# Attention values turned by DMA for the last six units, and q loaded in pairs of rows: one step in a chunked-attention and bilinear-FFN kernel

## The chip, the cores and the metric

One core of a Trainium2 chip runs the whole program in one launch. The metric is device time in microseconds (us). The kernel before was timed three times.

## The reference

The program computes attention inside chunks of 64 tokens, and feeds it to a bilinear feed-forward layer. All inputs and the output are float32; the kernel computes in bfloat16 with float32 sums.

```python
batch, n_heads, seq, head_dim = (8, 8, 576, 64)
chunk = 64; nc = S // chunk; scale = 1.0 / np.sqrt(D)
# q_c, k_c, v_c = q, k, v reshaped to (B, H, nc, chunk, D)
scores = scale * np.matmul(q_c, k_c.transpose(0, 1, 2, 4, 3))
scores = scores - np.max(scores, axis=-1, keepdims=True)
attn = np.exp(scores)
attn = attn / (np.sum(attn, axis=-1, keepdims=True) + 1e-09)
out = np.matmul(attn, v_c)                     # back to (B, H, S, D)
x = out.transpose(0, 2, 1, 3).reshape(B * S, H * D)   # 4608 tokens x 512
return (x @ w_a) * (x @ w_b) @ w_out           # 512 -> 1536 -> 512
```

## The kernel before

The 4608 tokens are cut into 9 blocks of 512 tokens (K = 0 to 8) and 18 units of 256 tokens (u = 0 to 17, two to a block, four chunks of 64 to a unit). Block 4 collects the last chunk of every sequence, so its tokens lie apart in DRAM; in the other blocks a unit is 256 tokens of one sequence.

**Attention of a unit.** `load_natural` (line 449) fetches q, k and v as tokens by heads, in DRAM runs of 64 float32 (256 bytes), two loads of 128 tokens to each tensor. `cast_natural` and `cast_v` make bfloat16 of them. One DMA transpose on SP (`turn_dma`, line 652) turns q and k of a unit, 128 x 2048 elements, into `qkT`, with head columns on partitions. Three pieces of TensorE (PE) work follow, all as 64 x 64 tiles of the PE array, four side by side:

- `part_scores` (line 781): 32 matmuls with a chunk of k as the weights and a chunk of q as the moving operand, and two exponentials on ScalarE (ACT) that write `E`.
- `part_sums` (line 739): four matmuls of 512 columns with a matrix of ones, which spread the sum of each softmax row over 64 partitions; ACT then takes the logarithm of both halves (line 745) and the exponential of its negative (line 747), which gives `inv`, the reciprocals.
- `part_values` (line 752): 32 matmuls with v as the weights and `E` moving. The product has model columns on partitions and tokens along the free dimension, as the FFN wants it, and VectorE (DVE) multiplies it by `inv` straight into `xT` (line 772).

Units 0 to 3 go through functions of their own with pairs of heads (`load_pair`, `cast_pair`, `turn_pair` and so on).

**FFN of a block.** Block 0 is done plainly (`ffn`). Blocks 1 to 8 go through `side_group` (three groups to a block, lines 882 to 995), which replaces eight block products by seven with sums of operands: `x_sums` (line 864) adds and subtracts quarters of `xT`, `product` (line 907) makes four matmuls of 256 columns on weights or weight sums, and ACT, DVE and GpSimd (POOL) combine the results into `AB`. `out_seven` (line 1185) does the same for the last matrix, and `out_last` (line 1036) for block 8. `store` (line 1015) and `send` (line 1086) write the output, a store of 128 tokens at a time, on SP's DMA queue, or at the very end also on ACT's.

**Order.** Every step is an operation with its dependences in a `Planner`. Which engine takes it, in what order, and which of the eight PSUM banks it uses is written out by hand in one long table, `ORDER_OF_ALL` (line 85), that `follow` reads: `a` is PE, `b` ACT, `c` DVE, `d` POOL, `e` the SP queue; the digits after a colon are banks; `f` is a fill matmul on zeros that only keeps PE running. The program order in the functions is thus not the order on the engines. In the table the 64-row work of the units stands in groups of adjacent steps between the FFN products; between the two kinds PE changes its tiling mode.

From block 5 on (`JOINT`), `attend_two` (line 1436) hands out the attention of two units at three places inside `out_seven`: sums of the first with scores of the second; values of the first with sums of the second; values of the second with scores of the next.

## Time and profile before

| | |
|---|---|
| median of three runs | 292.86 us (292.47 to 293.28) |
| the profiled execution | 292.49 us |
| its span, first to last instruction | 290.7 us |
| granted TensorE clock | 1.000 |
| busy: PE, DVE, POOL, ACT | 285.5, 246.2, 185.9, 176.2 us |
| DMA moved | 55.09 MB in 137176 packets, 122160 of them under 512 bytes |

The span is shorter than the time by what lies before the first and after the last instruction. A busy share says how long an engine had work, not whether that work set the end; for that one reads which engine the last chain runs through, and the timeline.

### The profile page before, as it was taken

What the parts mean: (1) busy time and instruction counts of PE and PEld (TensorE: products, weight loads), DVE (VectorE), ACT (ScalarE), POOL (GpSimd) and SP (SyncE); (2) the same over time, 40 slices, a digit from 0 to 9 for tenths busy, and PEclk for the clock granted to TensorE, in tenths of its full rate; (3) what the DMA queues carried; (4) which work ended last, traced back from release to release, by engine and by line L of the source; (5) the groups of instructions that cost most, each with busy time, mean ns of one, the idle gap of its engine ahead of it and who ended that gap; (6) DMA issues with size and microseconds to landing.
All of it is one profiled execution on the core that took longest, in us unless ns stands there. A gap on an engine that the chain in (4) does not pass through costs nothing.

```text
span 290.7 us, 8704 instructions
## 1 busy us (share of the span) xinstructions
PE 285.5 (98%) x3549; PEld 233.4 (80%) x3549; DVE 246.2 (85%) x433; ACT 176.2 (61%) x307; POOL 185.9 (64%) x180
## 2 busy tenths in 40 slices
PE   7999999999999999999999999999999999999995
PEld 3455458887887888788888878888888888888884
DVE  2778899998999998998988988779988889688583
ACT  3887977966667654866683496558827642332521
POOL 4641338465498298539899879967743685787530
PEclk9999999999999999999999999999999999999999
DMA  7999999899767899976999997997950120012034
GB/s 252 390 398 402 288 297 317 195 244 236 177 132 176 226 242 208 271 167 153 211 244 191 251 220 211 205 243 166 160 116 2 40 106 2 0 68 79 3 145 145
DMA packets 137176, 55.09 MB, mean 189 GB/s; under 512 B 122160, under 2 KB 128432, under 8 KB 137136
## 3 DMA queue, kind: packets, MB, share of 16 engines
q1 hardware_dynamic: 135904, 53.43, 71.9%
q10 hardware_dynamic: 1232, 1.11, 1.1%
q8 instruction: 27, 0.44, 0.6%
q14 instruction: 13, 0.11, 0.1%
HBM read 37.75 MB, written 9.44 MB: 162 GB/s over the span
## 4 chain that ended last, share of the span: by engine, by line
PE 95%; DMA 3%; DVE 0%; POOL 0%; issue 0%; ACT 0%; ACTq 0%
PE F L911 51%; PE F L1216 25%; PE F L822 7%; DMA f<-in_k_dram 3%; PE F L1054 3%; PE F L685 2%; PE F L723 2%; PE F L695 2%; PE F L1529 1%; PE F L501 1%; PE F L630 0%; PE F L579 0%; PE F L673 0%; PE F L550 0%; PE F L710 0%; POOL qkb L326 0%
## 5 line engine op out<-in xcount | busy, mean ns | idle before, releaser
L326 ACT COPY part<-F 128x512 f32<-128x512 f32 x91 | 52.5, 591 | 52.0 <-PE F L911 36.2
L945 POOL TENSOR_TENSOR AB<-AB,bsb 128x512 bf16<-128x512 bf16 x46 | 52.8, 1155 | 21.0 <-DVE wst L1173 7.2
L949 DVE TENSOR_TENSOR bsb<-F,part 128x512 bf16<-128x512 f32 x72 | 49.1, 684 | 8.0 <-PE F L911 4.8
L1173 POOL TENSOR_TENSOR wst<-AB 128x512 bf16<-128x512 bf16 x30 | 34.3, 1155 | 13.4 <-PE F L1216 9.9
L911 PEld LDWEIGHTS <-WA 128*128 128x128 bf16 x384 | 37.1, 98 | 5.5 <-issue 1.1
L911 PEld LDWEIGHTS <-WB 128*128 128x128 bf16 x384 | 37.6, 98 | 4.6
L326 ACT COPY wst<-F 128x512 f32<-128x512 f32 (+1 forms) x40 | 22.1, 557 | 29.7 <-PE F L1216 17.9
L949 DVE TENSOR_TENSOR AB<-F,part 128x512 bf16<-128x512 f32 x48 | 32.8, 684 | 2.0 <-PE F L911 1.4
L1216 PEld LDWEIGHTS <-wst 128*128 128x128 bf16 x288 | 28.0, 98 | 3.7 <-issue 0.4
L1216 PEld LDWEIGHTS <-AB 128*128 128x128 bf16 x288 | 28.1, 98 | 3.5 <-issue 0.2
L911 PEld LDWEIGHTS <-Tb 128*128 128x128 bf16 x288 | 27.6, 98 | 3.9 <-issue 0.5
L911 PEld LDWEIGHTS <-Ta 128*128 128x128 bf16 x288 | 27.7, 98 | 3.6 <-issue 0.3
L911 PE MATMUL F<-wst,Tb 128*128 128x256 bf16 x192 | 28.9, 273 | 0.0
L911 PE MATMUL F<-wst,Ta 128*128 128x256 bf16 x192 | 28.9, 273 | 0.0
L911 PE MATMUL F<-xT,WA 128*128 128x256 bf16 x192 | 28.9, 273 | 0.0
L911 PE MATMUL F<-wst,WA 128*128 128x256 bf16 x192 | 28.8, 273 | 0.0
L911 PE MATMUL F<-wst,WB 128*128 128x256 bf16 x192 | 28.8, 273 | 0.0
L911 PE MATMUL F<-xT,WB 128*128 128x256 bf16 x192 | 28.3, 273 | 0.0
L326 POOL CAST qkb<-f 128x1024 bf16<-128x1024 f32 (+1 forms) x21 | 17.2, 835 | 15.1 <-DVE Tb L859 6.3
L1216 PE MATMUL F<-WO,AB 128*128 128x256 bf16 x192 | 24.6, 273 | 0.0
L326 DVE COPY part<-F 128x512 f32<-128x512 f32 x29 | 19.8, 686 | 2.7 <-PE F L911 2.3
L772 DVE TENSOR_TENSOR xT<-F,inv 128x512 bf16<-128x512 f32 x28 | 18.0, 684 | 2.6 <-ACT inv L747 2.1
(135 smaller groups left out, 561.2 us busy)
## 6 DMA issues: line engine op xcount, KB each, us to landing
f<-in_q_dram SPq DMA_DIRECT2D x32, 256.0 KB, 4.8
f<-in_v_dram SPq DMA_DIRECT2D x32, 256.0 KB, 4.3
f<-in_k_dram SPq DMA_DIRECT2D x28, 256.0 KB, 4.5
out_dram<-osb SPq DMA_DIRECT2D x28, 256.0 KB, 3.2
wst<-in_moe_w_b_dram SPq DMA_DIRECT2D x6, 512.0 KB, 8.4
wst<-in_moe_w_a_dram SPq DMA_DIRECT2D x6, 512.0 KB, 8.7
wst<-in_moe_w_out_dram SPq DMA_DIRECT2D x6, 512.0 KB, 6.1
out_dram<-osb SPq DMA_DIRECT2D x12, 128.0 KB, 2.4
```

Of the source, the lines that this page charges most:

```text
L326: return A.copy(out=out, in_=in_) if e == "act" else ENG[e].tensor_copy(out=out, in_=in_)
L685: T.matmul(PS[j][cl * 64:cl * 64 + 64, c:c + 64], chunk_of(u, 1, m, j, 2 * g + cl), chunk_of(u, 0, m, j, 2 * g + cl), start=True, stop=True,)
L695: T.matmul(SU[cl][j * 64:j * 64 + 64, :], ones[cl * 64:cl * 64 + 64, :], E[u % 2][cl * 64:cl * 64 + 64, j, :], start=True, stop=True,)
L723: T.matmul(PA[cl][j * 64:j * 64 + 64, c:c + 64], vb[u % 2][cl * 64:cl * 64 + 64, g * 512 + h * 64:g * 512 + h * 64 + 64], E[u % 2][cl * 64 ...
L772: op("dve", c_dve(512), lambda e, cl=cl: V.tensor_tensor(out=x.rearrange("p m (g c t) -> p c g m t", g=2, c=2)[:, cl], in0=f_of(PA[cl]).re ...
L822: T.matmul(f_of(b)[:, 0:n].rearrange("p (u t) -> p u t", u=len(us)), w[ft][:, kt, :], x[:, us[0]:us[-1] + 1, kt, :], start=(kt == 0), stop ...
L911: T.matmul(f_of(bank)[:, q * 256:q * 256 + 256], lhs(2 * g + q, kt), rhs[:, kt, :], start=(first and q == 0 and kt == 0), stop=(q == 1 and ...
L945: op(("dve", "pool"), TIMES, lambda e: ENG[e].tensor_tensor(out=dst, in0=dst, in1=b, op=MULT), r=bk, w=key, prio=-300, fast=True)
L949: op("dve", c_dve(512), lambda e: V.tensor_tensor(out=dst, in0=two(f_of(bank)), in1=two(pab[s][i]), op=ADD), r=[("ps", id(bank)), ("part", ...
L1054: T.matmul(f_of(bank)[:, 0:256], lhs[:, i, h], rhs[:, i, :], start=(first and i == 0), stop=(i == NP - 1), skip_group_check=True)
L1173: op(*long_op(hs), lambda e, i=i, x=x, y=y, o_=o_: ENG[e].tensor_tensor(out=SS[i][:, s], in0=x[:, s], in1=y[:, s], op=o_), r=fts + [(name, ...
L1216: T.matmul(f_of(bank)[:, at:at + 256], lhs[:, i, tt * 128:tt * 128 + 128], rhs[:, i, :], start=(first and at == 0 and i == 0), stop=(i == ...
```

## The change

Two edits, and an order written anew.

1. For units 12 to 17 (`FROM = 12`, blocks 6 to 8) `part_sums` and `part_values` give way to `part_first` and `part_second`, each for half of the heads. The operands are swapped: a chunk of `E` is the weights and v is moving, so the product has tokens on partitions and model columns along the free dimension. `vb` gets a 65th column of ones beside each head's 64, so each matmul has 65 columns and the last is the sum of the softmax row. DVE takes the reciprocal of four sums to a partition and multiplies 256 columns by them into `xk`, which lies in the memory of `inv`; that is four reciprocals and four products to a unit. When both units of a block are done, `turn_x` turns 128 x 2048 elements into `xT` by one DMA transpose on SP. The tokens of a unit then stand in another order inside `xT` (chunk of the pair outermost), and `rows_of` writes them back in place: a store of 128 partitions goes to two groups of 64 rows in DRAM, 128 rows apart.
2. For units 4 to 17 q is loaded with two neighbouring tokens to a partition (`load_paired`), in DRAM runs of 512 bytes and in one load to a unit (four in block 4). The cast puts the two tokens in two halves of `qkb`, the same DMA transpose turns it, and `chunk_of` reads a chunk's 64 columns of q as 32 pairs, the two of a pair 512 elements (1,024 bytes) apart. k and v are loaded as before.
3. `ORDER_OF_ALL` is another table from its fifth step on. Steps by engine, before and after: PE without fills 580 and 580, ACT 311 and 298, DVE 432 and 460, POOL 172 and 175, SP 192 and 183, fills 25 and 24. The order of the first dozen loads on SP is the same.

The diff without the table and without lines that only rename:

```diff
@@ -215,7 +215,8 @@
     STORES = {}
     ORDER = "P0 P1 P2 P3 V0 V1 X0 q2 k2 X1 v2 X2 k3 q3 v3 O0 O1 O2 O3 O4 O5"
     JP = (0,4,7)
-    INVERSES = 2
+    FROM = 12
+    PAIRED = {(u, 0) for u in range(4, 18)}
     QT = 2
     JOINT = 4
     JOINT_SPARE = 1
@@ -271,22 +272,23 @@
 
     f32 = [[buf(f"f32_{i}_{x}", [128, 1024], FP32) for x in range(3)] for i in range(NF32)]
     qkb = [buf(f"qkb_{i}", [128, 2, 1024], BF16) for i in range(2)]
-    vb = [buf(f"vb_{i}", [128, 1024], BF16) for i in range(2)]
+    vb = [buf(f"vb_{i}", [128, 16, 66], BF16) for i in range(2)]
     qkT = [buf(f"qkT_{i}", [128, 16, 128], BF16) for i in range(QT)]
+    rec = [buf(f"rec_{i}", [128, 4, 4], FP32) for i in range(2)]
     E = [buf(f"E_{i}", [128, 2, 512], BF16) for i in range(2)]
 
     part = buf("part", [128, 3, 512], FP32)
-    inv = [buf("inv", [128, 2, 512], FP32), part[:, 0:2]] + [buf(f"inv_{i}", [128, 2, 512], FP32) for i in range(INVERSES - 1)]
-
-    def NI(u):
-
-        return 0 if u % INVERSES == 0 else 2
     xT = [buf(f"xT_{i}", [128, 2, NKT, 256], BF16) for i in range(NX)]
     AB = [buf(f"AB_{i}", [128, NP, 2, BLK], BF16) for i in range(2)]
     NB = 8
     bsb = buf("bsb", [128, NB, BLK], BF16)
     NO = 3
     osb = [buf(f"osb_{i}", [128, 2, DM], FP32) for i in range(NO)]
+    inv = [buf("inv", [128, 2, 512], FP32), part[:, 0:2], buf("inv_1", [128, 2, 512], FP32)]
+    xk = [inv[2 * i].rearrange("p a b -> p (a b)").bitcast(BF16).rearrange("p (u c) -> p u c", u=2) for i in range(2)]
+
+    def NI(u):
+        return 0 if u % 2 == 0 else 2
 
     WA = buf("WA", [128, NFT, NKT, 128], BF16)
     WB = buf("WB", [128, NFT, NKT, 128], BF16)
@@ -446,6 +451,27 @@
             return [(0, 128, b0, s0)]
         return [(0, 64, b0, s0), (64, 64, b1, s1)]
 
+    def load_paired(u, x, src):
+
+        t = f32[u % NF32][x].rearrange("p (h c) -> p h c", h=H)
+        (b, s0), (b1, _) = chunks[4 * u], chunks[4 * u + 1]
+        if b == b1:
+            load(t, src[b, :, s0:s0 + 256, :].rearrange("h (p r) d -> p h (r d)", r=2), f_keys(u, x), (1024, 24.0))
+            return
+        for n in range(4):
+            b, s0 = chunks[4 * u + n]
+            load(t[32 * n:32 * n + 32], src[b, :, s0:s0 + 64, :].rearrange("h (p r) d -> p h (r d)", r=2), f_keys(u, x, n), (256, 24.0))
+
+    def rows_of(u, tt, cols):
+
+        if u < FROM:
+            return [(p, n, out[b * S + s0:b * S + s0 + n, cols]) for p, n, b, s0 in runs(u, tt)]
+        (b0, s0), (b1, s1) = chunks[4 * u + tt], chunks[4 * u + 2 + tt]
+        if b0 == b1 and s1 == s0 + 128:
+            r0 = b0 * S + s0 - 64 * tt
+            return [(0, 128, out[r0:r0 + 256, cols].rearrange("(g c t) d -> c g t d", g=2, c=2)[tt])]
+        return [(64 * g, 64, out[b * S + s0:b * S + s0 + 64, cols]) for g, (b, s0) in enumerate(((b0, s0), (b1, s1)))]
+
     def load_natural(u, x, src, prio=None):
         t = f32[u % NF32][x]
         for g in range(2):
@@ -603,7 +629,7 @@
 
     def cast_v(u, engs, prio):
         cost = {"dve": 0.69, "pool": 1.04, "act": 1.05}
-        op(engs, [cost[e] for e in engs], lambda e: copy(e, vb[u % 2], f32[u % NF32][2]), r=f_keys(u, 2), w=vb_keys(u % 2), prio=prio, fast=True)
+        op(engs, [cost[e] for e in engs], lambda e: copy(e, vb[u % 2][:, :, 0:64], f32[u % NF32][2].rearrange("p (n d) -> p n d", n=16)), r=f_keys(u, 2), w=vb_keys(u % 2), prio=prio, fast=True)
 
     def v_rows(K, half):
         return osb[K].rearrange("p t c -> p (t c)").bitcast(BF16)[:, half * 1024:half * 1024 + 1024]
@@ -640,25 +666,37 @@
                 hs = (half,) if K in BY_HALF else (0, 1)
                 c = slice(256 * hs[0], 256 * hs[-1] + 256)
                 n = 256 * len(hs)
-                op(("act", "dve"), (c_act(n), c_dve(n)), lambda e, g=g, c=c: copy(e, vb[g // 2][:, g % 2 * 512:g % 2 * 512 + 512][:, c], f_of(VB[g])[:, c]),
+                op(("act", "dve"), (c_act(n), c_dve(n)), lambda e, g=g, c=c, hs=hs: copy(
+                    e, vb[g // 2][:, g % 2 * 8 + 4 * hs[0]:g % 2 * 8 + 4 * hs[-1] + 4, 0:64], f_of(VB[g])[:, c].rearrange("p (h d) -> p h d", d=64)),
                    r=[("ps", id(VB[g]))], w=[("vb", g // 2, g % 2, h) for h in hs], ps=[VB[g]], prio=R0)
 
 
     def cast_natural(u, x, engs, prio):
         cost = {"dve": 0.69, "pool": 1.04, "act": 1.05}
-        op(engs, [cost[e] for e in engs], lambda e: copy(e, qkb[u % 2][:, x, :], f32[u % NF32][x]),
-           r=f_keys(u, x), w=[("qkb", u % 2, x, 0), ("qkb", u % 2, x, 1)], prio=prio, fast=True)
+        to, got = qkb[u % 2][:, x, :], f32[u % NF32][x]
+        if (u, x) in PAIRED:
+            to, got = to.rearrange("p (r h d) -> p h r d", r=2, h=H), got.rearrange("p (h r d) -> p h r d", r=2, h=H)
+        op(engs, [cost[e] for e in engs], lambda e: copy(e, to, got),
+           r=f_keys(u, x), w=[("qkb", u % 2, x, n) for n in range(4)], prio=prio, fast=True)
 
     def turn_dma(u, prio):
         return op("sp", 0.6, lambda e: SP.dma_start_transpose(out=qkT[u % QT], in_=qkb[u % 2].rearrange("p x c -> p (x c)")),
-           r=[("qkb", u % 2, x, n) for x in range(2) for n in range(2)],
+           r=[("qkb", u % 2, x, n) for x in range(2) for n in range(4)],
            w=[("qkT", u % QT, x, n) for x in range(2) for n in range(2)], land=(2048, 17.0), prio=prio)
+
+    def turn_x(K, prio):
+        i = K % 2
+        return op("sp", 0.6, lambda e: SP.dma_start_transpose(out=xT[K % NX].rearrange("p u k (g t) -> p (u k g) t", g=2), in_=xk[i].rearrange("p u c -> p (u c)")),
+           r=[("xk", i, u, n) for u in range(2) for n in range(4)],
+           w=[("xT", K % NX, u, m, cl) for u in range(2) for m in range(4) for cl in range(2)], land=(2048, 17.0), prio=prio)
 
     TWO = TWO_UNITS
     SEVEN = SEVEN_BLOCKS
 
     def chunk_of(u, x, m, j, c):
         t = qkT[u % QT][j * 64:j * 64 + 64, 8 * x:8 * x + 8, :]
+        if (u, x) in PAIRED:
+            return t.rearrange("q (r m) p -> q m p r", r=2)[:, m, 32 * c:32 * c + 32]
         return t[:, 4 * (c // 2) + m, (c % 2) * 64:(c % 2) * 64 + 64]
 
     def mm_scores(u, PS):
@@ -722,19 +760,61 @@
                         h = 2 * m + j
                         T.matmul(
                             PA[cl][j * 64:j * 64 + 64, c:c + 64],
-                            vb[u % 2][cl * 64:cl * 64 + 64, g * 512 + h * 64:g * 512 + h * 64 + 64],
+                            vb[u % 2][cl * 64:cl * 64 + 64, g * 8 + h, 0:64],
                             E[u % 2][cl * 64:cl * 64 + 64, j, c:c + 64],
                             start=True, stop=True,
                         )
 
+    def part_turned(half):
+
+        def part(u, prio):
+            PA = P.bank("F"), P.bank("F")
+            keep.extend(PA)
+            K = u // 2
+            old = [P.ops[n] for x in range(2) for cl in range(2) for n in P.readers.get(("inv", 2 * (K % 2), x, cl), ())]
+            ms = range(2 * half, 2 * half + 2)
+
+            def pe():
+                for m in ms:
+                    for j in range(2):
+                        for g in range(2):
+                            for cl in range(2):
+                                c, n = g, 2 * (m % 2) + j
+                                T.matmul(
+                                    f_of(PA[cl])[c * 64:c * 64 + 64, n * 65:n * 65 + 65],
+                                    E[u % 2][cl * 64:cl * 64 + 64, j, g * 256 + m * 64:g * 256 + m * 64 + 64],
+                                    vb[u % 2][cl * 64:cl * 64 + 64, g * 8 + 2 * m + j, 0:65],
+                                    start=True, stop=True,
+                                )
+
+            def post():
+                for cl in range(2):
+                    i = 2 * half + cl
+
+                    def got(cl=cl):
+                        return f_of(PA[cl])[:, 0:260].rearrange("p (m j e) -> p m j e", m=2, j=2)
+
+                    op("dve", 0.19, lambda e, got=got, i=i: V.reciprocal(out=rec[u % 2][:, i].rearrange("p (m j) -> p m j", m=2), in_=got()[:, :, :, 64]),
+                       r=[("ps", id(PA[cl]))], w=[("rec", u % 2, i)], ps=[PA[cl]], prio=prio)
+                    op("dve", c_dve(256), lambda e, got=got, i=i, cl=cl: V.tensor_tensor(
+                        out=xk[K % 2][:, u % 2].rearrange("p (m s j d) -> p m s j d", m=4, s=2, j=2)[:, ms.start:ms.stop, cl], in0=got()[:, :, :, 0:64],
+                        in1=rec[u % 2][:, i].rearrange("p (m j) -> p m j", m=2).unsqueeze(3).to_broadcast([128, 2, 2, 64]), op=MULT),
+                       r=[("ps", id(PA[cl])), ("rec", u % 2, i)], w=[("xk", K % 2, u % 2, i)], ps=[PA[cl]], prio=prio, after=old)
+
+            return 0.138, pe, e_keys(u) + vb_keys(u % 2), PA, [], post
+
+        return part
+
+    part_first, part_second = part_turned(0), part_turned(1)
+
     def t_keys(u):
         return [("qkT", u % QT, x, n) for x in range(2) for n in range(2)]
 
     def e_keys(u):
         return [("E", u % 2, n, j) for n in range(2) for j in range(2)]
 
-    def i_keys(u):
-        return [("inv", NI(u), n, cl) for n in range(2) for cl in range(2)]
+    def i_keys(u, *cls):
+        return [("inv", NI(u), n, cl) for n in range(2) for cl in cls or range(2)]
 
     def part_sums(u, prio):
         SU = P.bank("F"), P.bank("F")
@@ -1014,9 +1094,8 @@
 
     def store(K, u, tt, t, key, prio, cols=(0, DM), eng="sp"):
         queue = {"sp": SP, "act": A}[eng]
-        for p, n, b, s0 in runs(2 * K + u, tt):
-            r0 = b * S + s0
-            op(eng, 0.55, lambda e, p=p, n=n, r0=r0: queue.dma_start(out=out[r0:r0 + n, cols[0]:cols[1]], in_=t[p:p + n, tt, cols[0]:cols[1]]),
+        for p, n, to in rows_of(2 * K + u, tt, slice(*cols)):
+            op(eng, 0.55, lambda e, p=p, n=n, to=to: queue.dma_start(out=to, in_=t[p:p + n, tt, cols[0]:cols[1]]),
                r=key, land=(n * len(range(*cols)) // 512, 90 if n == 128 else 175), prio=prio)
 
     def last_parts(K):
@@ -1426,8 +1504,13 @@
     def attend(u):
 
         unit_in(u + 2)
-        slot(AT + u + 0.5, (part_sums, u))
-        slot(AT + u + 0.6, (part_values, u))
+        if u < FROM:
+            slot(AT + u + 0.5, (part_sums, u))
+            slot(AT + u + 0.6, (part_values, u))
+        else:
+            slot(AT + u + 0.6, (part_first, u), (part_second, u))
+            if u % 2:
+                turn_x(u // 2, -60 + u)
         if u == 3:
             value_in(4)
         value_in(u + 2)
@@ -1440,15 +1523,24 @@
 
         def one():
             unit_in(u + 2)
-            slot(AT + u, (part_sums, u), (part_scores, u + 1), fixed=True)
+            if u < FROM:
+                slot(AT + u, (part_sums, u), (part_scores, u + 1), fixed=True)
+            else:
+                slot(AT + u, (part_scores, u + 1), fixed=True)
 
         def two():
             unit_in(u + 3)
-            slot(AT + u + 0.5, (part_values, u), (part_sums, u + 1), fixed=True)
+            if u < FROM:
+                slot(AT + u + 0.5, (part_values, u), (part_sums, u + 1), fixed=True)
+            else:
+                slot(AT + u + 0.5, (part_first, u), (part_second, u), fixed=True)
             value_in(u + 2)
 
         def three():
-            slot(AT + u + 1, (part_values, u + 1), (part_scores, u + 2), fixed=True)
+            values = ((part_values, u + 1),) if u < FROM else ((part_first, u + 1), (part_second, u + 1))
+            slot(AT + u + 1, *values, (part_scores, u + 2), fixed=True)
+            if u >= FROM:
+                turn_x(u // 2, -60 + u)
             value_in(u + 3)
 
         return one, two, three
@@ -1530,6 +1622,8 @@
     })
     with tc.manual_schedule():
         V.memset(ones, 1.0)
+        for x in vb:
+            V.memset(x[:, :, 64:66], 1.0)
         make_identity(nc, identity)
         G.memset(picks, 0.0)
         G.affine_select(out=picks, in_=picks, pattern=[[-1, 515]], compare_op=mybir.AluOpType.not_equal, fill=1.0, base=3, channel_multiplier=4)
```

More of the change, by code (lines that the diff above doesn't have):

```diff
@@ L371, in load_pair, with v_keys @@
         ))
+    def v_keys(i, *ns):
+        return [("f32", i, 2, n) for n in ns]
     def load_v0(half, K=0):
@@ L387, in load_v0 @@
                 v[K, :, g * 128:(g + 1) * 128, :].transpose([1, 0, 2]),
-                [("f32", half, 2, 2 * n + i) for i in range(2)], (1024, VNS), issue=0.55,
+                v_keys(half, 2 * n, 2 * n + 1), (1024, VNS), issue=0.55,
             )
@@ L474, in cast_pair @@
             f32[hu][x][:, mm * 512:mm * 512 + 512].rearrange("p (h r d) -> p h r d", h=2, r=4),
[L475 removed]
+        ), r=[("f32", hu, x, mm)], w=[("qkb", hu, x, n) for n in ((0,), (1, 2, 3))[mm]], prio=R0 + m if prio is None else prio, fast=True)
     keep = []
```

198 lines of the change are left out of this document (98 added, 100 removed).

## The prediction

> **What bounds the kernel now.** I read the page of the profile first: the span, the busy shares and the chain that ended last.
>
> ```profile
> core 0: 290.7 us, clock 1.000
> PE 285.5 (98%) x3549; PEld 233.4 (80%) x3549; DVE 246.2 (85%) x433; ACT 176.2 (61%) x307; POOL 185.9 (64%) x180
> PE 95%; DMA 3%; DVE 0%; POOL 0%; issue 0%; ACT 0%; ACTq 0%
> ```
>
> The profiled execution took 292.49 us by the clock, so 1.8 us lie outside its span. It is 0.37 us under the median of the three runs (292.86), and I carry the sum over to the median at the end. TensorE holds 95% of the chain. A busy PE is not yet a full PE, so next the windows by stage.
>
> ```profile
> core 0: us, PE busy (x) PEld busy (x) DVE busy (x) ACT busy (x) POOL busy (x), PEclk, DMA share, GB/s
> 7.00:17.50 10.50, 10.29 (x220) 5.71 (x219) 8.69 (x16) 8.92 (x26) 6.51 (x11) 1.00 1.08 392
> 17.50:53.00 35.50, 35.48 (x359) 21.32 (x352) 31.71 (x59) 28.75 (x48) 15.34 (x15) 1.00 1.06 334
> 144.00:231.00 87.00, 87.00 (x1186) 75.00 (x1186) 74.80 (x128) 56.86 (x96) 66.73 (x61) 1.00 0.81 174
> 280.00:290.70 10.70, 7.45 (x69) 6.44 (x66) 4.97 (x13) 2.02 (x6) 1.15 (x1) 1.00 0.50 180
> ```
>
> From 17.5 us on PE is never idle until the tail. The stretch 144 to 231 us holds the attention of the last six units, which the change rewrites; there DVE is busy 74.8 of 87 us and ACT 56.9. Whether PE's time there is dense shows in the timeline, where the distance from one start to the next is what a piece costs.
>
> ```profile
> start us, us, engine line op out<-in xcount [idle before <-releaser]
> 119.58 0.44 PE L685 MATMUL F<-qkT 64*64 64x64 bf16 x32
> 119.85 0.39 PE L695 MATMUL F<-E,ones 64*64 64x512 bf16 x4
> 120.17 0.39 PE L1216 MATMUL F<-WO,AB 128*128 128x256 bf16 x2
> 202.40 0.60 PE L911 MATMUL F<-wst,Ta 128*128 128x256 bf16 x4
> 202.83 0.60 PE L911 MATMUL F<-wst,WB 128*128 128x256 bf16 x4
> 203.36 0.63 PE L695 MATMUL F<-E,ones 64*64 64x512 bf16 x8
> 203.92 0.61 PE L911 MATMUL F<-wst,WA 128*128 128x256 bf16 x4
> 207.08 0.71 PE L723 MATMUL F<-E,vb 64*64 64x64 bf16 x64
> 207.73 0.39 PE L911 MATMUL F<-wst,Ta 128*128 128x256 bf16 x2
> ```
>
> Four products of 256 columns start every 0.43 us (202.40, 202.83), and around 64-row work that becomes 0.53 (202.83 to 203.36): a change of mode costs about 0.1 us on each side. Nothing else is lost. So the time is the sum of what PE is given, and what other engines save counts only if they begin to hold PE up, or stop doing so.
>
> **The change part by part.**
>
> *The sums of units 12 to 17 go.* Two units' sums with the way out of the mode take 0.56 us (203.36 to 203.92), one unit's 0.32 (119.85 to 120.17); the difference, 0.24 us, is one unit's four matmuls. Six units make -1.44 us, all on the path. The changes of mode do not go: in the old written-out order the work of these units stands in nine groups between products, and in the new one too (nine runs of adjacent two-bank steps), because the values are now cut in halves. Had three groups gone as well it would be another 0.6 us.
>
> *The values turned.* Per unit still 32 matmuls of 64 rows, now with 65 columns in place of 64. The old 64 for two units take 0.65 us with the way out (207.08 to 207.73); one column in 64 on 0.27 us for 32 is 0.004 us a unit, +0.02 in all.
>
> *The elementwise work around them* is off the path.
>
> ```profile
> L745 ACT ACTIVATE inv<-F 128x512 f32<-128x512 f32 x32 | 17.6, 608 | 3.2 <-PE F L695 3.2
> L747 ACT ACTIVATE inv<-inv 128x1024 f32<-128x1024 f32 x16 | 16.8, 1071 | 0.2
> L772 DVE TENSOR_TENSOR xT<-F,inv 128x512 bf16<-128x512 f32 x28 | 18.0, 684 | 2.6 <-ACT inv L747 2.1 <-PE F L723 0.3
> L592 DVE TENSOR_TENSOR xT<-F,inv 128x256 bf16<-128x256 f32 x4 | 1.4, 416 | 0.0
> L560 DVE RECIPROCAL inv<-F 128x256 f32<-128x256 f32 x2 | 3.5, 1748 | 0.0
> ```
>
> ACT loses 2 x 608 + 1071 = 2287 ns a unit, 13.7 us in all. DVE trades 2 x 684 for four products of 256 at 416 ns and four reciprocals of four columns. From 684 and 416 the part that does not grow with the columns is about 0.15 us; 1748 ns for 256 columns is then 6.2 ns a column, so a reciprocal of four is about 0.18 us. That is 4 x 0.60 = 2.4 us against 1.37, +1.0 a unit and +6.2 us in all. The new order gives DVE 28 steps more, not the 36 that the change adds, so about 8 steps of some 0.6 us move to ACT and GpSimd, and DVE stays near its 86% of this stretch. ACT's freed time covers it; without that cover DVE would need 6.2 us inside 87, which it still has (12.2 idle). Price 0, bounds -0.3 (ACT waited for L695 3.2 us in 16 units, which held others little) and +1 (below).
>
> *q in 512-byte runs.* 14 units. The loads run beside a full PE, so they are worth nothing on the path; SP issues 12 loads fewer. What lies on the path is the other end: each score matmul now reads its 64 columns of q from two places 1,024 bytes apart in turn. The trace has no matmul that reads so. The nearest rows are strided reads by other engines:
>
> ```profile
> L326 ACT COPY part<-F 128x512 f32<-128x512 f32 x91 | 52.5, 591 | 52.0 <-PE F L911 36.2 <-DVE AB L949 8.1 <-DVE bsb L949 3.9
> L326 ACT COPY qkT<-F 128x512 bf16<-128x512 bf16 x11 | 6.2, 586 | 3.1 <-PE F L501 3.1
> ```
>
> The copies into qkT read four places 256 bytes apart in turn (line 509), the copies into part read straight, and they take 586 and 591 ns: a stride costs ACT nothing. I take 0 for PE from that row, though it is another engine and PSUM. The upper bound is a halved rate: four sum matmuls side by side need 0.24 us for 512 columns (119.85 row above), so 64 columns are 0.03 us, and 8 fours x 14 units x 0.03 = +3.4 us.
>
> The Trainium skill ("Advanced Engine Details and Errata", section "SBUF Cachelines") says that SBUF is read in lines of 16 bytes, that full rate needs at least two hits in a line, and that every step to another line costs. By that the sum would take the +3.4 and not the 0. No run here shows it.
>
> *Three transposes and the fill.* Each block of the last three gets its FFN input by one DMA transpose on SP once all eight products of a block are written.
>
> ```profile
> 39.66 0.38 PE L1529 MATMUL F<-zero 128*128 128x512 bf16 x1
> 39.97 0.74 PE L710 MATMUL F<-E,vb 64*64 64x64 bf16 x64
> 211.04 0.68 DVE L772 TENSOR_TENSOR xT<-F,inv 128x512 bf16<-128x512 f32 x1
> 212.37 1.16 POOL L871 TENSOR_TENSOR wst<-xT 128x512 bf16<-128x512 bf16 x1 [0.36 <-DVE AB L945]
> qkT<-qkb SPq DMA_TRANSPOSE x14, 4.2
> ```
>
> A transpose of this size lands 4.2 us after its issue; it needs no engine but SP, and behind it on SP wait loads and stores that are not urgent. In the old order the first product on block 7's values stands 12 PE steps (6.2 us) after its values, and the summing on GpSimd starts 0.65 us after DVE's last write (211.72 to 212.37). With the transpose that becomes some 5 us more, so the new order must have moved the values earlier or the products later. It is written out anew from one end to the other, so I price this at 0, up to +2 for one block that comes short. The one fill matmul in the dense stretch (39.66 to 39.97) is gone in the new order, 24 fills for 25; that is 0 to -0.3, and I take -0.1, since it may have covered a wait. The order of the first loads is unchanged, so the start stays.
>
> **Sum.** 292.49 - 1.44 + 0.02 - 0.1 = 290.97 us in terms of the profiled run, 291.3 in terms of the median. With the bounds of the small terms, 290.5 to 292.0.
>
> **The rivals.**
>
> *Scores at half rate (slower).* The terms above with +3.4: 291.3 + 3.4 = 294.7 us, 293.8 if only part of the reading is exposed. It decides from 1.5 us, that is from 13 ns in each of the 112 fours. For it: nothing else in the kernel feeds PE so, and the four have no slack (0.27 us for 32 in the row at 119.58). Against it: the strided rows of ACT.
>
> *The last three blocks' stores on two DMA engines (much slower).* The token order inside a unit changes, so a store of 128 rows goes to two groups of 64 rows in DRAM. If the transfer is divided by the outermost step of its destination, that was 128 rows and becomes 2, and two engines do the work of sixteen.
>
> ```profile
> DMA packets 144, 0.26 MB, mean 131 GB/s; under 512 B 16, under 2 KB 16, under 8 KB 144
> q1 hardware_dynamic: 144, 0.26, 33.9%
> out_dram<-osb SPq DMA_DIRECT2D x1, 256.0 KB, 2.0
> 278.71 3.32 SPq L1019 DMA_DIRECT2D out_dram<-osb  x4
> q1 hardware_dynamic: 1728, 2.03, 44.2%
> q10 hardware_dynamic: 144, 0.07, 1.8%
> ```
>
> The first three lines are the window 255 to 257 us, with one store: 128 data packets and 16 small ones, one for each engine; 33.9% of 16 engines for 2 us is 10.8 engine-us. The last two are the window 278 to 290.7, with the stores of blocks 7 and 8: 46.0% of 12.7 us of 16 engines is 93.5 engine-us. On two engines that is 46.7 us; begun at about 279.5 - 1.5, and with 1.3 us after the last packet, the span would end near 326 and the run at 328 us. For it: sixteen small packets to a store show that the work is split by engines. Against it: no row shows by what it is split, and a split by partition would leave all sixteen.
>
> The Trainium skill ("DMA: Bandwidth & Descriptors", section "Why a DMA increments its semaphore by 16 and not by 1") states such a rule, the largest number up to 16 that divides the slowest dimension of both sides. The sixteen small packets of a 128-row store agree with it; they agree with a split by partition as well.
>
> *New waits.* Some groups now take six of the eight PSUM banks at once, and DVE needs 4 x 0.60 us for a unit in place of 1.37 before the banks are free; or a transpose comes late. Nine such places at 0.1 to 0.3 us, or one late block at 2 us: 291.8 to 294.
>
> **How the numbers follow.** A measurement of this kernel can tell about 0.3% from no change, 0.9 us: faster means below 292.0, slower above 293.7. Forecast 0.40; half rate 0.18; two engines 0.28, the mechanism with the largest price and no row that excludes it; new waits 0.14, of which 0.04 faster, 0.05 same, 0.05 slower. Of the forecast's chance 0.02 falls within 0.3%. Faster 0.38 + 0.04 = 0.42; same 0.02 + 0.05 = 0.07; slower 0.18 + 0.28 + 0.05 = 0.51. The likeliest single case is the forecast, 291.3, own range 290.5 to 292.0. Without the two-engine case more than 2 in 10 would be left out, so the range goes from 290.4 to 328.5.
>
> **What would show it.** In the changed profile: 40 sum matmuls of 512 columns and not 64; score groups of 32 still 0.27 us from start to start (half rate: 0.5); ACT about 10 us less busy; DVE up by a few; PE still without idle time from 17.5 us; a store of block 7 with 16 small packets and landing in about 2 to 3 us (two engines: 2 packets, over 6 us, and DMA work long after the last matmul). I am wrong if the scores stretch, if the span ends far from the last matmul, or if PE shows idle time named for DVE or for the transposed xT.

## The result, and the profile after

The changed kernel takes 330.84 us (median of 4 runs, 330.51 to 330.86) against 293.07 us for the kernel before on the same chip (292.47 to 294.36): a ratio of 1.128, 95% interval 1.1241 to 1.1319. The forecast was 291.3, the range ended at 328.5. The time lies above the range, and the sign of the forecast was wrong.

First the page of the changed kernel: the span, the engines' busy time, the slices of PE and of the DMA engines, and the chain that ended last.

```profile
span 329.0 us, 8665 instructions
PE 287.2 (87%) x3522; PEld 235.4 (72%) x3524; DVE 245.7 (75%) x463; ACT 170.4 (52%) x294; POOL 188.9 (57%) x183
PE   7999999999999999999999999999999999830000
DMA  7999999996888999398593898991040011011111
PE 77%; DMA 8%; DVE 1%; ACT 1%; SPq 1%; issue 0%; POOL 0%; DVEq 0%
```

PE is as busy as before (287.2 us for 285.5), but it is done four slices before the end, and in those slices the DMA engines show a 1, a tenth of their sixteen. Its last matmul starts at 290.71 us of the span (287.18 before). So of the 38.3 us that the span grew, 3.5 came while PE worked and 34.8 after it. The windows say the same and add the sum of the dense stretch:

```profile
core 0: us, PE busy (x) PEld busy (x) DVE busy (x) ACT busy (x) POOL busy (x), PEclk, DMA share, GB/s
144.00:231.00 87.00, 87.00 (x1192) 75.67 (x1191) 74.81 (x148) 47.95 (x81) 67.82 (x62) 1.00 0.78 187
291.00:329.00 38.00, 0.00 (x0) 0.00 (x0) 0.42 (x1) 0.00 (x0) 0.00 (x0) 0.55 0.13 48
```

In the last 38 us DMA works alone, but for one DVE instruction, at 0.13 of sixteen engines, which is two of them, and at 48 GB/s. (PE has no work there, so its clock of 0.55 explains nothing.) The stretch 144 to 231 has PE at 87.00 of 87.00, as before: the transposes and the new DVE work cost nothing there.

What the DMA engines do in the tail, from the view of transfers for 285 to 329 us, and how long SP needs to issue them, from SP's timeline:

```profile
DMA packets 1642, 2.05 MB, mean 47 GB/s; under 512 B 26, under 2 KB 1130, under 8 KB 1642
```

```profile
257.24 10.08 SPq L1098 DMA_DIRECT2D out_dram<-osb  x4
284.48 5.78 SPq L1098 DMA_DIRECT2D out_dram<-osb  x3
290.36 9.16 SPq L1168 DMA_DIRECT2D out_dram<-f  x1
317.26 2.59 SPq L1168 DMA_DIRECT2D out_dram<-osb  x1
```

26 small packets for 13 stores: two to a store, where the kernel before had sixteen. And SP, which mostly issued such a store in 0.33 to 0.44 us before, now stands up to 9.16 us in one issue, so that the last one is issued at 317 us. Each store shares its two engines with all stores ahead of it: the share stays at 0.13 though several are under way.

Then PE's own 3.5 us. Its timeline around 118 us, first one row of the kernel before, whose next product starts at 117.95, then the changed kernel:

```profile
117.57 0.45 PE L685 MATMUL F<-qkT 64*64 64x64 bf16 x32
```

```profile
118.08 0.69 PE L723 MATMUL F<-qkT 64*64 64x64 bf16 x32
118.70 0.61 PE L991 MATMUL F<-xT,WB 128*128 128x256 bf16 x4
122.75 0.69 PE L723 MATMUL F<-qkT 64*64 64x64 bf16 x32
123.27 0.42 PE L761 MATMUL F<-E,vb 64*64 64x64 bf16 x32
```

A score group of 32 now holds PE for 0.52 us before 64-row work (122.75 to 123.27) where it was 0.27, and 0.62 before a product (118.08 to 118.70) where it was 0.38: +0.24 us in each of 14 units, 3.4 us. The groups of instructions and PE's waits give the rest:

```profile
L733 PE MATMUL F<-E,ones 64*64 64x512 bf16 x40 | 4.0, 390 | 0.0
L797 DVE RECIPROCAL rec<-F 128x4 f32<-128x4 f32 x24 | 3.4, 166 | 0.5 <-PE F L783 0.4
L799 DVE TENSOR_TENSOR inv<-F,rec 128x256 bf16<-128x256 f32 x24 | 9.3, 415 | 0.3
```

```profile
PE F L1294 <- DVE osb L1322: 0.9, 1, 0.9
DVE osb L1322 <- DMA out_dram<-osb: 1.1, 1, 1.1
```

40 sum matmuls for 64, so -1.44 us as summed; and one stall of 1.06 us at 280.48 in the trace (the view of waits counts 0.9 of it), in which PE waits for DVE, and DVE for an output buffer `osb` whose store is still on its two engines. 3.4 - 1.44 + 1.06 is 3.0. The rest is small: eight waits of 0.05 to 0.24 us between PE's products, from 51.6 to 266.0 us of the trace, are 0.8 us in sum (the kernel before has one of 0.05 there), and the fill that is gone takes off 0.3. That makes about 3.5.

So two things that the prediction had as separate rivals came true at once, with some small waits beside them. The experiments ask first whether each of the two is what it seems.

### The profile page after: what moved, and what is told of

It is laid out like the page before. It is cut to its first block, busy times and chain, and to the rows that moved or that the text cites. A ratio compares the mean times of both kernels' runs of the same rounds, so it can differ in the third digit from the quotient of the medians.

```text
span 329.0 us, 8665 instructions
## 1 busy us (share of the span) xinstructions
PE 287.2 (87%) x3522; PEld 235.4 (72%) x3524; DVE 245.7 (75%) x463; ACT 170.4 (52%) x294; POOL 188.9 (57%) x183
## 4 chain that ended last, share of the span: by engine, by line
PE 77%; DMA 8%; DVE 1%; ACT 1%; SPq 1%; issue 0%; POOL 0%; DVEq 0%
PE F L991 40%; PE F L1294 20%; PE F L902 6%; DMA out_dram<-osb 6%; PE F L723 2%; PE F L1133 2%; DMA f<-in_q_dram 1%; PE F L527 1%; DMA f<-in_v_dram 1%; PE F L1621 1%; PE F L733 1%; PE F L761 1%; PE F L783 1%; SPq L1098 0%; PE F L576 0%; PE F L656 0%
## 5 line engine op out<-in xcount | busy, mean ns | idle before, releaser
L328 ACT COPY part<-F 128x512 f32<-128x512 f32 x93 | 53.3, 588 | 58.1 <-PE F L991 32.9
L1025 POOL TENSOR_TENSOR AB<-AB,bsb 128x512 bf16<-128x512 bf16 x45 | 51.8, 1157 | 21.2 <-DVE AB L1025 5.8
L328 ACT COPY wst<-F 128x512 f32<-128x512 f32 (+1 forms) x38 | 21.3, 565 | 33.4 <-PE F L1294 10.8
L328 POOL CAST qkb<-f 128x512 bf16<-128x512 f32 (+1 forms) x22 | 17.9, 825 | 13.1 <-DVE WA L328 3.7
L1251 POOL TENSOR_TENSOR spare_sum<-AB,wst 128x512 bf16<-128x512 bf16 x16 | 18.5, 1155 | 8.7 <-DVE AB L1025 4.8
L328 DVE COPY part<-F 128x512 f32<-128x512 f32 x27 | 18.5, 686 | 4.2 <-PE F L991 2.7
```

Of the source, the lines that this page charges most:

```text
L328: return A.copy(out=out, in_=in_) if e == "act" else ENG[e].tensor_copy(out=out, in_=in_)
L1025: op(("dve", "pool"), TIMES, lambda e: ENG[e].tensor_tensor(out=dst, in0=dst, in1=b, op=MULT), r=bk, w=key, prio=-300, fast=True)
L1251: op(*long_op(hs), lambda e, i=i, x=x, y=y, o_=o_: ENG[e].tensor_tensor(out=SS[i][:, s], in0=x[:, s], in1=y[:, s], op=o_), r=fts + [(name, ...
```

## The stores alone, and what divides a store

**The kernel before with stores as the kernel after has them.**

```diff
-queue.dma_start(out=out[r0:r0 + n, cols], in_=...)
+to = out[r0:r0 + 256, cols].rearrange("(g c t) d -> c g t d", g=2, c=2)[tt]   # units 12 to 17
+queue.dma_start(out=to, in_=...)
```

> The kernel before with one thing changed: the stores of units 12 to 17 go to two groups of 64 rows, 128 rows apart, as the kernel after has them (the rows of the output of these units thus stand in another order). If the outermost step of a destination decides on how many engines a store runs, the tail of the kernel after appears without any of its other edits: 93.5 engine-us for blocks 7 and 8 on two engines, some 46 us after about 278 us, a time of 326 to 330 us. Rival: the division goes by partitions, and the tail has another cause: 293 us, stores landing in 2 us.

Measured: 326.98 us in one run, 33.8 us over the kernel before (293.21 in the shared runs). Its window 285 to 325 us:

```profile
DMA packets 1596, 1.90 MB, mean 48 GB/s; under 512 B 26, under 2 KB 1178, under 8 KB 1596
```

Same tail, without transposes, paired reads or a new table. Its span is 325.2 us; the rival's working said 326, with 1.5 us taken off for the sums, which this kernel still has, so 327.5 like for like. The destination of the stores is the cause of the tail.

**Six stores with six outermost steps**, in the kernel before:

```diff
+OUTER = {(5, 1, 0): 64, (5, 0, 0): 2, (6, 1, 0): 4, (6, 1, 1): 8, (6, 0, 0): 16, (6, 0, 1): 32}
+to = to.rearrange("(a b) d -> b a d", b=many)
```

> The kernel before; six stores of 128 rows, one each, have a destination whose outermost step is 64 and 2 (the stores of block 5's second and first half named here), and 4, 8, 16, 32 (block 6), so that rows of the output of these stores stand in other places. If a store runs on as many engines as the largest number up to 16 that divides the outermost step, the store of 2 has 2 small packets and lands about 5.4 us of transfer later (10.8 engine-us on 2), that of 4 after 2.7, of 8 after 1.4, and those of 16, 32 and 64 after 0.7, as every other store with 16 small packets. If partitions decide, all have 16 small packets and land alike, about 2 us after issue. The time of the kernel: 293 us either way, since the stores of these blocks end long before the end.

Measured: 293.9 us. The small packets in the trace, in windows that hold the end of one store or two: 226.5 to 231 (step 64), 239.2 to 243 (step 2), 255.5 to 261 (step 8), 268 to 270 (step 4):

```profile
DMA packets 144, 0.26 MB, mean 58 GB/s; under 512 B 16, under 2 KB 16, under 8 KB 144
...
DMA packets 61, 0.12 MB, mean 31 GB/s; under 512 B 4, under 2 KB 4, under 8 KB 61
...
DMA packets 137, 0.28 MB, mean 51 GB/s; under 512 B 8, under 2 KB 8, under 8 KB 136
...
DMA packets 48, 0.09 MB, mean 45 GB/s; under 512 B 4, under 2 KB 4, under 8 KB 48
```

16, 8 and 4 engines for steps of 64, 8 and 4, and between 260.5 and 274 us 36 small packets for steps of 32, 16 and 4, that is 16 + 16 + 4. Fewer engines take longer: the last small packet of the store of step 2 comes 7.6 us after its issue, that of step 8 after 3.7 and that of step 4, which stood behind two other stores, after 6.4; the stores of 16, 32 and 64 landed after 2.4 to 2.8. The second window needs care. Two of its four small packets (240.88 and 240.94 us) end the store of step 2; the other two (241.52, 241.59) belong to the plain store issued behind it, whose other fourteen had ended by 239.14. That plain store landed 7.8 us after its issue, where the one of step 64 landed after 2.4 (issues in the windows 226.5 to 231 and 234.5 to 243 us):

```profile
out_dram<-osb SPq DMA_DIRECT2D x1, 256.0 KB, 2.4
...
out_dram<-osb SPq DMA_DIRECT2D x1, 256.0 KB, 7.8
```

So a store on few engines also holds up its successor, whose shares on those engines queue behind it. A division by partitions is ruled out: all six stores have 128. The rule of the Trainium skill ("DMA: Bandwidth & Descriptors", section "Why a DMA increments its semaphore by 16 and not by 1"), the largest number up to 16 that divides the slowest dimension of both sides, gives 16, 2, 4, 8, 16, 16; the trace agrees in all six.

**The kernel after with each such store issued as two of 64 adjacent rows.**

```diff
-queue.dma_start(out=to, in_=src[p:p + n, cols])
+for g in range(2):
+    queue.dma_start(out=to[g], in_=src[p + 64 * g:p + 64 * g + 64, cols])
```

> The kernel after, with one thing changed: a store of 128 partitions in units 12 to 17 is issued as two stores of 64 partitions, each to one group of 64 adjacent rows in DRAM. If the destination's outermost step (2 groups) is what puts a store on two DMA engines, each half now has 64 steps and goes to sixteen: the tail shrinks to 1 to 2 us after the last matmul and the time falls from 330.8 to 294 to 295 us (last matmul at 290.7 in the changed trace, plus 1.3 for the last store, plus 1.8 outside the span, less up to 1.1 for the stall of TensorE at 280 us). Score groups of 32 stay at 18.3 ns a matmul. Rival: the tail comes from the number of stores or from late issue on SP; then more issues make it longer, 330 us or above.

Measured: 300.94 us, ratio to before 1.0263 (1.0237 to 1.0288). 29.9 us of the tail are gone, but 6 more stayed than expected. SP's timeline:

```profile
282.50 5.02 SPq L479 DMA_DIRECT2D out_dram<-osb  x8
295.48 1.18 SPq L479 DMA_DIRECT2D out_dram<-osb  x2
```

5.02 us for eight: each of these issues of 64 rows takes SP 0.54 to 0.60 us, more than one of 128 rows. From 281.3 to 296.7 us SP does little else; the last matmul starts at 289.49, the last issue at 296.07. The expectation had counted data and not issues, though the trace of before has the price: its stores of 64 rows around 202 us, from the block whose tokens lie apart, take SP 0.57 to 0.66 us each.

**The first half of each issued by ACT.**

```diff
-    queue.dma_start(out=to[g], ...)
+    (queue if g else A).dma_start(out=to[g], ...)
```

> The kernel with divided stores, with the first half of each issued by ACT and the second by SP. In the kernel with divided stores SP issues 26 stores of 64 rows without a break from 279 to 296 us, 0.54 to 0.60 us each, and the last 6.6 us after the last matmul. If the issue on one queue is what is left of the tail, two queues end it: 13 issues on each take 8 us, so the last is issued when its data is there, 1 to 2 us after the last matmul: 295 to 296.5 us (the upper end if ACT's copies wait behind the issues). Rival: the engines need longer for rows of 64, and the time stays at 300 us.

Measured: 304.30 us, 1.0365 (1.031 to 1.0419), 8 us above what was expected. The last issue does come 2.8 us after the last matmul (6.6 with one queue), so the queue on SP is gone, but the last matmul now starts at 296.18. ACT's timeline shows why:

```profile
283.33 4.04 ACTq L479 DMA_DIRECT2D out_dram<-osb  x4
287.76 0.37 ACT L328 COPY wst<-F 128x256 f32<-128x256 f32 x1 [5.58 <-DMA out_dram<-osb]
```

ACT's four issues start at 283.33, 284.60, 285.99 and 286.53 us, each when its data is there, and the copy that PE needs next stands behind them all. It took the time from one engine and gave it to one that was on the path.

## The scores: what a matmul pays for reading from places apart

**q as two runs of 32**, on the kernel with divided stores; ACT puts `E` back in order as it writes.

```diff
-return t.rearrange("q (r m) p -> q m p r", r=2)[:, m, 32 * c:32 * c + 32]
+return t.rearrange("q (r m) p -> q m r p", r=2)[:, m, :, 32 * c:32 * c + 32]
-A.activation(out=E[u % 2][:, j], in_=f_of(PS[j]), ...)
+A.activation(out=E[u % 2][:, j].rearrange("p (n t r) -> p n r t", n=8, r=2),
+             in_=f_of(PS[j]).rearrange("p (n r t) -> p n r t", n=8, r=2), ...)
```

> As the kernel with divided stores, and the scores read q's 64 columns of a chunk as two runs of 32 adjacent columns (even tokens, then odd ones) in place of 32 pairs 1,024 bytes apart; the exponential on ACT writes E back in the order of tokens through a stride of two. If reading in pairs costs TensorE, the score matmuls go back from 18.3 to 10.3 ns in the profile and the time is 3.5 us under the kernel with divided stores: about 291 us. If the loads in rows of 512 bytes or the casts cost it, nothing changes: 294 to 295 us. Cost of the strided write on ACT: between 0 (its strided copies take 586 and 591 ns) and a doubled write, 28 x 0.5 us beside other work.

Measured: 298.48 us, 1.0182 (1.0155 to 1.0209): 2.5 us under its partner (300.94), and the score groups are back at 0.27 and 0.38 us. Loads in 512-byte rows and casts are the same in both kernels, so the reading is the cause. Of the 3.4 us PE got 2.6 (last matmul 286.89 for 289.49). Small stalls came in their place: at 92.3, 119.0 and 144.9 us PE loses 0.25, 0.10 and 0.20 us that it does not lose with divided stores alone, each time before a sum matmul, which reads `E`. The rows of ACT and PE for the last of them:

```profile
143.89 1.35 ACT L874 ACTIVATE E<-F 128x512 bf16<-128x512 f32 x2
145.29 0.41 PE L740 MATMUL F<-E,ones 64*64 64x512 bf16 x4
```

The second exponential ends at 145.24 us and the sums start at 145.29 (at 92.49 and 92.54, 119.24 and 119.29 in the other two places). The scores are done earlier now, and ACT's exponential, writing through a stride, takes longer (730 ns for 599), so PE meets it.

**Other columns of q in the kernel before**, by unit:

> The kernel before; the scores of some units read other columns of q than their own, so that the 64 columns of a matmul lie: units 4 and 5 every second element (4 bytes apart), 6 every 4th (8 bytes), 7 every 8th (16), 8 every 16th (32), 9 in pairs 1,024 bytes apart as in the kernel after, 10 and 11 in pairs 64 bytes apart, 12 and 13 two adjacent elements every 32 bytes, 16 and 17 two runs of 32, and 14 and 15 as before. Theory (lines of 16 bytes, full rate with two reads in a line): 0.27 us from start to start for 32 matmuls in units 4, 5, 6, 12, 13, 16, 17 and 14, 15; about 0.5 in 7, 8, 9, 10, 11. Rival a: every stride of one element halves it (4 to 11 slow, 12 to 17 fast). Rival b: only the distance of 1,024 bytes costs it (only 9 slow), with something like banks behind it. Time 293 to 295 us.

Measured: 295.22 us. The score groups of PE's timeline in the order of units 4 and 5, 6, 7, 8, 9, 10 and 11, 12 and 13, 14 and 15, 16 and 17:

```profile
62.64 0.73 PE L698 MATMUL F<-qkT 64*64 64x64 bf16 x64
88.43 0.65 PE L698 MATMUL F<-qkT 64*64 64x64 bf16 x32
90.21 1.11 PE L698 MATMUL F<-qkT 64*64 64x64 bf16 x32
118.52 1.11 PE L698 MATMUL F<-qkT 64*64 64x64 bf16 x32
121.19 0.69 PE L698 MATMUL F<-qkT 64*64 64x64 bf16 x32
143.32 1.19 PE L698 MATMUL F<-qkT 64*64 64x64 bf16 x64
170.87 1.13 PE L698 MATMUL F<-qkT 64*64 64x64 bf16 x64
202.29 0.71 PE L698 MATMUL F<-qkT 64*64 64x64 bf16 x64
220.16 0.73 PE L698 MATMUL F<-qkT 64*64 64x64 bf16 x64
```

**More patterns, in the same way:**

> The kernel before; scores of some units read other columns than their own: units 4 and 5 alternate between two places 1,024 bytes apart after every 2 columns, 6 after every 4, 7 after every 8, 8 after every 16, 9 reads runs of 4 columns 32 bytes apart, 10 and 11 every third element, 16 and 17 runs of 8 columns 32 bytes apart, 14 and 15 as before; 12 and 13 read the weights (k) every 16th element instead. Theory A, from the first set of reads: what counts is the number of reads in one line of 16 bytes before the line changes; four are enough. Then the change after 2 costs as the step of 8 bytes did (13 to 14 ns a matmul), after 4, 8 and 16 nothing (8.3 ns), runs of 4 and 8 nothing, every third element about 10 ns. Theory B: what counts is an even number of adjacent columns; then change after 2 is free too. Weights: no expectation of either; 8.3 ns if their loading stays hidden.

Measured: 294.33 us; the groups in the same order (units 8, 9, 14 to 17 are left out, they read 0.45 for 32 and 0.71 and 0.73 for 64):

```profile
62.62 0.77 PE L697 MATMUL F<-qkT 64*64 64x64 bf16 x64
88.45 0.44 PE L697 MATMUL F<-qkT 64*64 64x64 bf16 x32
90.02 0.45 PE L697 MATMUL F<-qkT 64*64 64x64 bf16 x32
...
141.55 0.93 PE L697 MATMUL F<-qkT 64*64 64x64 bf16 x64
168.84 2.11 PE L697 MATMUL F<-qkT 64*64 64x64 bf16 x64
```

The rows hold the end of the last matmuls too; from the first start to the last, divided by the steps between, a matmul costs:

| 64 columns of the moving operand read | ns each |
|---|---|
| adjacent; every 2nd; two runs of 32; runs of 4 or 8, 32 bytes apart | 8.2 to 8.3 |
| every 3rd element (6 bytes) | 11.5 |
| every 4th (8 bytes); runs of 2, 32 bytes apart | 13.5; 14.2 |
| every 8th (16 bytes); every 16th (32 bytes) | 26.2; 26.4 |
| two places in turn, change after each column, 1,024 or 64 bytes apart | 15.2; 15.3 |
| two places in turn, change after 2; after 4, 8 or 16 columns | 9.1; 8.1 to 8.2 |
| weights (k) every 16th element, q adjacent | 29.1 |

The distance of the two places is nothing (rival b falls), and not every stride halves the rate (rival a falls: every 2nd is free). The cost is flat from 16 bytes on and gone at four reads to 16 bytes. That is the line of 16 bytes of the Trainium skill ("Advanced Engine Details and Errata", section "SBUF Cachelines"), which asks for at least two hits in a line; two are not yet full rate here, 13.5 and 14.2 ns, where four take 8.3. Counted by the stretches of 16 bytes that 64 columns of q touch, 64 of them cost 26.2 to 26.4 ns, 32 of them 13.5 to 14.2, 24 of them 11.5, and 16 or fewer nothing beyond the 8.3: 0.41 to 0.48 ns for each. That is three times the adjacent rate at 16 bytes, where the expectation had a halved one. Reading two places in turn fits neither of the theories of the second set: after each column it costs 15.2 and not the 26 of a new line each time, after two columns 9.1 and not 14. Why turning back is cheaper than going on to a new stretch stays open.

## The first edit alone, and whole stores again

**q loaded, cast and read as before**, on the kernel with divided stores (256-byte runs, two loads to a unit, in the place of the paired ones):

```diff
-load(t, src[b, :, s0:s0 + 256, :].rearrange("h (p r) d -> p h (r d)", r=2), ...)
+for g in range(2):
+    SP.dma_start(out=t[:, g], in_=src[b, :, s0 + 128 * g:s0 + 128 * g + 128, :].transpose([1, 0, 2]))
```

> As the kernel with divided stores, but q loaded, cast and read as in the kernel before: 256-byte runs, two loads to a unit, adjacent columns. What is left is the first edit with whole stores: values as tokens by columns, sums beside them, the transpose by DMA. By the sum of the prediction it stands 1.4 to 1.5 us below the kernel before: 291 to 291.6 us, with score matmuls at 10.3 ns and 40 sum matmuls of 512 columns. Rival: the first edit brings waits of its own that eat the 1.44 us, 292.5 to 294; then TensorE's idle time shows them.

Measured: 297.81 us, 1.0162 (1.0134 to 1.0189). The expectation of 291 to 291.6 shared the mistake on the issues of half stores; the tail is in this kernel as well. So the stores had to be whole.

**Tokens in order within a unit**, three kernels. For the second pair of chunks scores and v stand on the other half of the partitions, and each pair gets a bank of its own:

```diff
+p = cl ^ g                      # scores of units 12 to 17 write E on half p
-f_of(PA[cl])[c * 64:c * 64 + 64, ...], E[u % 2][cl * 64:cl * 64 + 64, ...], vb[u % 2][cl * 64:cl * 64 + 64, ...]
+f_of(PA[g])[cl * 64:cl * 64 + 64, ...], E[u % 2][p * 64:p * 64 + 64, ...], vb[u % 2][p * 64:p * 64 + 64, ...]
-return [(0, 128, out[r0:r0 + 256, cols].rearrange("(g c t) d -> c g t d", g=2, c=2)[tt])]
+return [(p, n, out[b * S + s0:b * S + s0 + n, cols]) for p, n, b, s0 in runs(u, tt)]
```

> The kernel after, with the tokens of units 12 to 17 put in order within a unit: for the second pair of chunks the scores and v stand on the other half of the partitions (v of that pair comes in two loads of 64 rows), and the values of each pair of chunks go to one bank, so a store of 128 partitions is again 128 adjacent rows, one DMA with outermost step 128. Scores still read q in pairs. Theory (both costs, two engines and issue of half stores, lie in the stores' form): the last store ends about as long after the last matmul as in the kernel before (5.3 us from the last matmul to the end of the run), so 289.5 + 5.3 = 294.8 us, 294.3 to 295.2. Rival: the 6.6 us that the kernel with divided stores still has between its last matmul and its last issue come from the order on SP, not from the number of issues; then about 300.

> The same with q read as two runs of 32 adjacent columns. Theory: 286.9 + 5.3 = 292.2 us, 2.5 us under the kernel with rows in order alone, and 0.2 to 0.4% under the kernel before (293.2 in the shared runs). Rival: the gain of 1.44 us from the sums is eaten by waits; then 293 or above.

> The same rows in order, with q loaded, cast and read as in the kernel before: the first edit alone, with whole stores. The kernel with divided stores and this q had 297.8 us, 0.7 under its partner with runs of 32, so 291.5 us, 291.2 to 292.4, 1.0 to 2.0 us under the kernel before: the 1.44 us of the sums. Rival: 293 or above.

Measured, against 293.52 us of the kernel before in the shared runs:

| kernel | us | ratio to before, 95% |
|---|---|---|
| rows in order, q read in pairs | 294.70 | 1.0053 (1.0032 to 1.0073) |
| rows in order, q in two runs of 32 | 292.32 | 0.9966 (0.9948 to 0.9985) |
| rows in order, q as before | 292.52 | 0.9971 (0.9953 to 0.9990) |

The end of the second of them on SP, for the rows of the tails above:

```profile
281.08 2.19 SPq L1104 DMA_DIRECT2D out_dram<-osb  x3
287.44 0.33 SPq L1174 DMA_DIRECT2D out_dram<-f  x1
288.09 0.33 SPq L1174 DMA_DIRECT2D out_dram<-osb  x1
```

Single issues take 0.33 us again, the last one starts 0.8 us after the last matmul (287.33), as before. With the stores whole the change costs 0.5% through its reading of q; with that mended too it is 0.3% faster than the kernel before. The last two are both faster than before and after, and the same to what the runs can tell. So q's longer loads bring no gain that the runs can see, as summed; but the kernel that has them also has the stalls behind ACT's strided write (the same three, 0.55 us), so a gain of that size would be hidden.

## Why the prediction was wrong, by its steps

- *q's strided read at 0* failed. It was taken from ACT's copies, which read PSUM and not SBUF, and another engine's operand. The bound written beside it, 8 x 14 x 0.03 = 3.4 us, was met: 14 x 0.24. In time it is worth 2.4 (294.70 - 292.32), since stalls take its place when it goes: six of 0.10 to 0.48 us in the trace of the second kernel, 1.4 us in sum, that the first does not have.
- *The stores at 0* failed: the sum held nothing for them, and their destination was left to a rival at 0.28. The rival's working was good: a span of 327.5 without the gain of the sums, 325.2 measured where it acts alone. What spoke against it, "a split by partition would leave all sixteen", had no row either: nothing in the trace of before excluded the price. The rule of the Trainium skill that stood beside it ("DMA: Bandwidth & Descriptors", section "Why a DMA increments its semaphore by 16 and not by 1") gave two engines, and the trace agrees (26 small packets for 13 stores). It should have been the likeliest case.
- *The range* failed by adding each rival to the forecast alone. The two do not exclude each other: PE, behind by its slower reading, brings the first two-engine store to SP at 257.24 us, where the kernel with the stores alone has it at 254.64, and all later stores queue behind it. From measured parts, 326.98 + 3.5 is 330.5, and 330.84 was measured; the 2.3 us above the range are the second cost. That the rivals' own 328 + 3.4 = 331.4 comes as near is in part luck, since 328 was some 2 us too much for the stores.
- *A store prices its engines only* was short: the rival had no term for the buffers that slow stores hold (the stall of 1.06 us) nor for SP standing in its issues.
- *Sums, -1.44 us*: the 24 matmuls went. With stores and reading mended the kernel is 1.0 to 1.2 us faster (292.52 and 292.32 for 293.52), and the intervals reach 0.5 us to either side, so 1.44 is neither confirmed to the tenth nor contradicted. The eight waits of 0.05 to 0.24 us are what *new waits* had at 0.1 to 0.3 each; they came true beside the others and not in their place.
- *Transposes, DVE and ACT at 0*: right. PE is dense from 144 to 231 us; a reciprocal of four takes 166 ns (0.18 forecast) and a product 415. ACT is 5.8 us less busy, not 10, and DVE 0.5 less rather than a few more: more steps moved between the engines than were counted, beside the path.
- *What would show it* held: the stretched scores, a span that ends far from the last matmul, and two small packets to a store were named as the signs of being wrong.

## What to carry to other kernels

When a layout is turned, follow it to the last transfer: a store whose destination starts with a step of two runs on two engines, at 48 GB/s here, and neither its bytes nor its partitions show it. Price an access pattern by a row of the same engine and the same memory; where there is none, the bound is the price until a run says otherwise, and rivals that do not exclude each other are added up for the end of the range. To mend a pattern, look first at the place where data is made (which half of the partitions, which bank): here that cost one more load of v to a unit, off the path, while twice as many stores cost 6 us of issues at the end, and issues on a busy engine cost its work.

## What the runs showed of the hardware beyond that

- An issue of 64 rows takes SP longer than one of 128 adjacent rows: mostly 0.47 to 0.54 us for 0.33 to 0.37 as the first of a pair, and 0.59 to 0.60 for 0.42 to 0.44 right behind another. Why was not tried.
- A stall of PE can cost more than its length. In the kernel with ACT issuing stores, PE idled 2.3 us before 288.18 us, and the window behind it shows half the clock:

```profile
285.80:288.20 2.40, 0.10 (x2) 0.01 (x1) 0.16 (x1) 0.37 (x1) 0.00 (x0) 0.94 0.81 231
288.30:290.50 2.20, 2.20 (x12) 1.53 (x11) 0.42 (x1) 0.00 (x0) 0.00 (x0) 0.50 0.27 84
```

12 matmuls of 256 columns took 2.2 us there, where the same number starts within 1.3 us at full clock (0.43 us for four). The next stall of PE, 1.46 us before 292.36, shows no such loss: the clock from 292.3 to 296 us is 1.00. That a stall of 2.3 us brings the clock down is read from this one place.
- ACT's strided write is not free: its exponentials on `E` have a mean of 731 ns with 28 of 32 written through a stride of two elements, and 599 ns without. PE met it in three places, 0.55 us in sum (above).
